# Mamba-2 block and quick-GELU layer: float64 weights in 1024-byte runs, held transfers, code pages shifted by idle products, y in two parts, w_out stationary in one group

## Chip, cores, metric

One Trainium2 chip, one of its cores. The metric is the device time of one execution in microseconds (us). Lower is better.

## What is computed

Two layers. The first is a state-space (SSD) recurrence over 4 batches x 8 heads x 768 positions, head size 32, state size 16. The second is a feed-forward layer over the 3072 tokens that come out, 256 to 2048 to 256 wide, with h / (1 + exp(-1.702 h)) between. Cut to what matters:

```python
# per batch and head; x 32 wide, B and C 16 wide
state = decay * state + B[j] x[j]          # decay from a
y[i] = C[i] . state                        # (done by chunks)
x = y as (3072, 256)
h = x @ w_in                               # (256, 2048)
g = h * sigmoid(1.702 * h)
out = g @ w_out                            # (2048, 256)
```

`w_in` and `w_out` arrive as float64; everything else is float32. The kernel turns the float64 bits into float32 on the chip.

## The kernel before

**Tiling.** The 3072 tokens are six groups g = 0 to 5 of 512; a group is two pairs of 256 tokens (PG = 2). The title's counting begins at 1, the code's at 0: "group 1" is g = 0, "groups 2 and 3" are g = 1 and 2. Each group goes through: the SSD part for its two pairs (`decay`, `score`, `weigh`, `gain`, `keep_both`, `finish`, which leaves y in `yT`), the hidden layer (16 blocks f of 128 columns), and the projection.

**SSD names.** `decay(p)` scans the decays into `L` on DVE, from rows of a that `spread(p)` broadcasts from a scratch tensor in DRAM into a tile of the `bits` pool. `score` multiplies C and B into `cb` (PE, L666), `weigh` is L times cb (DVE, L677), `gain` makes the increments A of the state (PE, L697) from x and `Be`, and `finish` makes y: an inter-chunk part (PE, L787) and an intra-chunk part (PE, L799). Its two pieces are 64 and 128 small matmuls of at most 64 columns. The first group has forms of its own: `mask_banks` (L534), `differ` (L540), `decay_exp`, `since_first`, `parts_first`, `keep_first` (a scan on DVE, L721).

**Weights.** `PIECES` lists four pieces of w_in with 2 blocks, two with 4, and four of w_out with 4. `fetch(i)` brings one piece as raw 32-bit words into a tile of the `bits` pool (four buffers). DVE and ACT then make float32 of it: `fields` (two DVE operations, L188 and L191), `clamp` (two on ACT, L199 and L200), `rounded` (DVE, L204), `join` (two on DVE, L215 and L221; L221 writes `w_in` or `w_out`). `narrow(i)` is `rounded(i)`, `fields(i+1)`, `join(i)`.

**Group g = 0** is computed plainly: `hidden(0, f)` is two products of 128x512 (L846), `project_all` sums over f with gT stationary and w_out moving (L944), four products of 128x256 for each f, and two DVE operations (L950) scale the result for `store`. **From g = 1 on** both layers work on 2x2 blocks with seven products in place of eight: `first` (L902, L912) with the mixed tiles `mix_in` and `mix_y`, and `product` (L1009, L1016) with `mix_w` and `mix_g`; `combine` and `turn_out` (transposes on DVE, L1063) make the output. In g = 1 the first four hidden blocks are plain too (steps H0 and H1).

**Order.** The order of every engine is that of the code, pinned by `in_order`. It is written by hand: lists of steps such as `"2.1 3.1 2.5 ... y L"`, in which "j.i" is product i of block j, "P" the next product of the group before, "D", "S", "T" the DVE and ACT steps of a block, and other names call functions; and `at(places, f, ...)`, which puts work behind a block. All loads but a few of the first are issued from SP in that order, so a load that waits holds back what stands behind it on SP.

**Idle products.** `keep_busy(4, 20)` runs 20 products of 32x32 and 4 of 128x192 on constants before the first real ones. In `product`, for g = 1 the first 30 products run as two halves of 128 columns.

In the head, the SP order before is: a, C, B, `fetch(0)`, x of pairs 0 and 1, `fetch(1)` to `fetch(3)`, all of a (`rows_a`), `fetch(4)`, `fetch(5)`; later `load(PG)`, which is b, c and x of pair 2.

Of the kernel before, what the change touches and what calls it, by code (L numbers as in the profile page):

```python
# [16 lines left out]
P = 128  # L17
# [18 lines left out]
def kernel(  # L36
# [73 lines left out]
    w_in = const.tile([P, NK, DF], FP32, name="w_in")  # L110
    w_out = const.tile([P, NF, DM], FP32, name="w_out")
# [51 lines left out]
    def fetch(i):  # L163
        name, f, n = PIECES[i]
        if n == 2 and f % 4:
            t = pieces.pop(i - 1)[:, 2 * n * DM:]
        else:
            t = pieces[i] = words(f"bits{i}")
            t = t[:, :2 * n * DM]
        if name == "in":  # L170
            src = moe_w_in[:, 2 * f * P:2 * (f + n) * P].rearrange("(k p) e -> p k e", p=P)
            dst = t.rearrange("p (k e) -> p k e", k=NK)
        else:
            src = moe_w_out[f * P:(f + n) * P, :].rearrange("(f p) e -> p f e", p=P)
            dst = t.rearrange("p (f e) -> p f e", f=n)
        nc.sync.dma_start(out=dst, in_=src)
        t = t.rearrange("p (e w) -> p e w", w=2)
        bits[i] = t[:, :, 0], t[:, :, 1]
# [32 lines left out]
    def join(i):  # L211
# [5 lines left out]
        if name == "in":  # L217
            dst, split = w_in[:, :, f * P:(f + n) * P], NK
        else:
            dst, split = w_out[:, f:f + n, :], n  # L220
        nc.vector.scalar_tensor_tensor(  # L221
            out=dst, in0=m.bitcast(FP32).rearrange("p (k e) -> p k e", k=split),
            scalar=2.0 ** -20, in1=p2.bitcast(FP32).rearrange("p (k e) -> p k e", k=split),
# [14 lines left out]
    def spread(p):  # L238
# [3 lines left out]
        else:  # L242
            ra[p] = words(f"a{p}").bitcast(FP32)[:, :2 * NH * H].rearrange(
                "p (k e) -> p k e", k=2)
        b, c = divmod(2 * p, NC)
# [38 lines left out]
    for i in range(1, 4):  # L284
        fetch(i)
    rows_a(az, (nc.sync,))
    for i in range(4, 6):
        fetch(i)
# [47 lines left out]
    for k in range(2):  # L336
        fold_ident(k)
# [37 lines left out]
    whose = const.tile([32, 1 + PG, NH, N], FP32, name="whose")  # L375
    nc.gpsimd.memset(whose, 1.0)
    for t, head in ((whose[:, 1:], PG), (whose[:, :1], 1)):
        nc.gpsimd.affine_select(out=t, in_=t, pattern=[[-1, t.shape[1]], [-head, NH], [0, N]],
                                compare_op=ALU.is_equal, fill=0.0, base=0, channel_multiplier=1)
# [43 lines left out]
    def keep_busy(n, m):  # L423

        t = bank("busy")
        for i in range(m):
            c = 32 * (i % R)
            nc.tensor.matmul(out=t[c:c + 32, :32], lhsT=ones[:32, :32], rhs=ones[:32, :32],
                             start=True, stop=True, tile_position=(0, c), skip_group_check=True)
        for i in range(n):  # L430
# [58 lines left out]
    def fan_rows(t, c0, c1, o):  # L489

        o = o[:, :(c1 - c0) * P]
        nc.tensor.matmul(out=o, lhsT=whose[:, 0].rearrange("p h n -> p (h n)"),
# [4 lines left out]
    def since_first():  # L497

        since[0] = ssd.tile([P, NC, P], FP32, tag="since", name="since0")
        o = bank("rows0")  # L500
        for p in range(PG):
            nc.tensor.matmul(out=o[:, 2 * p * P:2 * (p + 1) * P],
                             lhsT=whose[:, 1 + p].rearrange("p h n -> p (h n)"),
                             rhs=cum[:32].rearrange("p k s -> p (k s)"), start=True, stop=True,
                             tile_position=(0, 0), skip_group_check=True)
        to = since[0][:, :CG]
        nc.scalar.activation(to.rearrange("p c s -> p (c s)"), o, AF.Exp)
        nc.gpsimd.tensor_copy(
            drop[:, :, 1:], to.rearrange("p c (s i) -> p (c s) i", s=2)[:, 1:, H - 1].unsqueeze(
                1).to_broadcast([P, Q * D, 2 * CG - 1]))  # L510

    def fan_since():
# [3 lines left out]
        nc.tensor.matmul(out=f, lhsT=whose[:, 0].rearrange("p h n -> p (h n)"),  # L516
# [244 lines left out]
    def finish(pairs):  # L761
# [4 lines left out]
        y = area(f"y{pairs[0]}")[:, :, :len(pairs) * 2 * H].rearrange(  # L766
            "p (s t) (k i) -> p s t k i", s=2, i=H)
        both, y = y, [y[:, i] for i in range(2)]
        begun = set()
# [45 lines left out]
        else:  # L815
            for part in inter, intra:
                for n, p in enumerate(pairs):
                    part(n, p)
# [21 lines left out]
    def hidden(g, f):  # L840
# [4 lines left out]
        for k in range(NK):  # L845
            nc.tensor.matmul(out=h, lhsT=w_in[:, k, f * P:(f + 1) * P], rhs=yT[g][:, k],  # L846
                             start=(k == 0), stop=(k == NK - 1))
# [6 lines left out]
    def mix_in(n):  # L854
# [3 lines left out]
        w = w_in[:, :, 4 * n * P:4 * (n + 1) * P].rearrange(  # L858
            "p k (j i e) -> p k j i e", j=2, i=2)
        a11, a12, a21, a22 = w[:, 0, :, 0], w[:, 1, :, 0], w[:, 0, :, 1], w[:, 1, :, 1]  # L860
# [20 lines left out]
    def first(g, j, i):  # L881
# [6 lines left out]
        A = w_in[:, :, 2 * j * P:2 * (j + 1) * P].rearrange("p k (i e) -> p k i e", i=2)  # L888
# [48 lines left out]
    def project_all(g, between):  # L937

        o = [bank(f"o{g}_{j}").rearrange("p (k e) -> p k e", k=2) for j in range(CG // 2)]
        for f in range(NF):  # L940
            for do in between.get(f, []):
                do()
            for k in range(CG):
                nc.tensor.matmul(out=o[k // 2][:, k % 2],  # L944
                                 lhsT=gT[g, f // 2][:, f % 2, k * P:(k + 1) * P],
                                 rhs=w_out[:, f], start=(f == 0 and k % 2 == 0),
                                 stop=(f == NF - 1), skip_group_check=True)
        for half in range(2):
            ob = out_tile(g, half)
            nc.vector.tensor_single_scalar(out=ob, in_=o[half], scalar=1.0 / GELU_SCALE,  # L950
                                           op=ALU.mult)
            store(g, half, ob)
# [429 lines left out]
```

## Time and profile before

| | us |
|---|---|
| median of 5 runs | 360.34 |
| lowest to highest | 357.21 to 363.61 |
| the profiled execution | 358.18 |
| its span, first to last instruction | 356.4 |
| mean granted TensorE clock | 0.986 |

The page is one execution. Times in it are us unless they are marked ns, counted from the first instruction. PE is TensorE, PEld its weight loads, DVE VectorE, ACT ScalarE, POOL GpSimd, SP the engine that issues most transfers. An fp32 product shows as two records on PE. "issue" is time in which an engine waited for nothing that the profile shows. q1 is the queue of SP's transfers, q8 carries instructions. The page's slices of 8.9 us:

```profile
PE   8589999999999999989999999999999999999996
DVE  6869997999696999677789285789384455465463
PEclk9959999999999999999999999999999999999999
DMA  5987399532655000476214503210000210000301
```

Each digit is a tenth of the slice. PE is busy nearly everywhere, the second and third slices apart, and in the third the granted clock is half. The transfers are thick in the first 60 us.

### The profile page before, as it was taken

How to read it: one execution, taken by the hardware profiler on the slowest of the kernel's cores; microseconds unless marked ns; L12 is line 12 of the kernel's file. 1: busy time of each engine (PE TensorE's matmuls, PEld its weight loads, DVE VectorE, ACT ScalarE, POOL GpSimd, SP SyncE). 2: the span in 40 equal slices, each digit the busy share in tenths (PEclk: the TensorE clock that was granted, in tenths of full speed). 3: DMA queues.
4: the chain of work that ended last, by engine and by line, in shares of the span. 5: the costliest groups of instructions: out<-in, count | busy, mean ns of one | idle time of the engine just before them, and what ended most of it. 6: DMA issues, size and time to landing. Idle time of an engine off the chain costs nothing.

```text
span 356.4 us, 8330 instructions
## 1 busy us (share of the span) xinstructions
PE 345.4 (97%) x3516; PEld 286.6 (80%) x3516; DVE 255.7 (72%) x476; ACT 148.0 (42%) x329; POOL 14.5 (4%) x40
## 2 busy tenths in 40 slices
PE   8589999999999999989999999999999999999996
PEld 6354448887679998868888888888888888889996
DVE  6869997999696999677789285789384455465463
ACT  4748756103363431635333445333444331453320
POOL 8400000100000100000000000000000000000000
PEclk9959999999999999999999999999999999999999
DMA  5987399532655000476214503210000210000301
GB/s 144 243 282 160 122 213 260 97 78 33 138 131 105 2 0 2 73 132 109 36 26 78 100 5 89 37 23 2 1 4 2 37 24 0 1 2 0 61 0 59
DMA packets 81533, 25.92 MB, mean 73 GB/s; under 512 B 69081, under 2 KB 75097, under 8 KB 81497
## 3 DMA queue, kind: packets, MB, share of 16 engines
q1 hardware_dynamic: 80824, 25.01, 32.0%
q8 instruction: 27, 0.44, 0.5%
q10 hardware_dynamic: 672, 0.39, 0.4%
q14 instruction: 10, 0.07, 0.1%
HBM read 22.15 MB, written 3.24 MB: 71 GB/s over the span
## 4 chain that ended last, share of the span: by engine, by line
PE 95%; DVE 2%; issue 1%; ACT 1%; DVEq 0%
PE acc L1009 27%; PE X L902 18%; PE Y L912 13%; PE h L846 11%; PE o L944 8%; PE acc L1016 7%; PE y L799 3%; PE y L787 2%; PE cb L666 2%; PE A L697 1%; PE busy L431 1%; DVE L L677 1%; PE ab L534 0%; PE ab L540 0%; DVE c L1040 0%
## 5 line engine op out<-in xcount | busy, mean ns | idle before, releaser
L907 ACT ACTIVATE ac<-X 128x256 f32<-128x256 f32 x76 | 29.1, 382 | 81.4 <-PE X L902 81.0
L1009 PE MATMUL acc<-mg,mw 128*128 128x256 f32 (+1 forms) x216 | 54.7, 356 | 0.0
L1036 DVE TENSOR_TENSOR gT<-Y,ac 128x512 f32<-128x512 f32 x38 | 26.2, 689 | 37.0 <-PE Y L912 32.7
L879 ACT ACTIVATE gT<-gT 128x512 f32<-128x512 f32 (+1 forms) x76 | 39.3, 520 | 32.3 <-DVE gT L1036 31.6
L902 PE MATMUL X<-my,mi 128*128 128x256 f32 x152 | 45.1, 380 | 0.0
L1009 PEld LDWEIGHTS acc<-mg,mw 128*128 128x128 f32 x216 | 39.0, 190 | 4.8
L1036 DVE TENSOR_TENSOR gT<-Y,b 128x256 f32<-128x256 f32 x38 | 15.9, 419 | 31.8 <-PE Y L912 31.8
L846 PE MATMUL h<-yT,w_in 128*128 128x512 f32 x80 | 37.7, 632 | 0.7 <-ACT yT L822 0.7
L1009 PE MATMUL acc<-gT,w_out 128*128 128x256 f32 (+1 forms) x148 | 35.6, 351 | 0.0
L846 PEld LDWEIGHTS h<-yT,w_in 128*128 128x128 f32 x80 | 16.1, 203 | 20.3 <-issue 18.1
L902 PEld LDWEIGHTS X<-my,mi 128*128 128x128 f32 x152 | 27.5, 190 | 3.2
L1009 PEld LDWEIGHTS acc<-gT,w_out 128*128 128x128 f32 x148 | 26.2, 190 | 3.2
L944 PE MATMUL o<-w_out,gT 128*128 128x256 f32 x128 | 28.5, 381 | 0.0
L870 DVE TENSOR_TENSOR mg<-gT 128x512 f32<-128x512 f32 x40 | 27.2, 681 | 0.0
L944 PEld LDWEIGHTS o<-w_out,gT 128*128 128x128 f32 x128 | 24.0, 190 | 3.3 <-issue 0.2
L902 PE MATMUL X<-yT,w_in 128*128 128x256 f32 x76 | 23.3, 390 | 0.0
L907 ACT ACTIVATE b<-X 128x256 f32<-128x256 f32 x38 | 14.6, 383 | 20.8 <-PE X L902 20.3
L912 PE MATMUL Y<-yT,mi 128*128 128x256 f32 x76 | 22.7, 381 | 0.3 <-DVE gT L1036 0.3
L912 PE MATMUL Y<-my,mi 128*128 128x256 f32 x76 | 22.7, 381 | 0.1
L912 PE MATMUL Y<-yT,w_in 128*128 128x256 f32 x76 | 22.6, 379 | 0.0
L902 PE MATMUL X<-my,w_in 128*128 128x256 f32 x76 | 22.5, 380 | 0.0
L397 DVE TENSOR_TENSOR_SCAN L<-a,idents 128x1024 f32<-128x1024 f32 x9 | 20.5, 2282 | 0.0
(151 smaller groups left out, 545.2 us busy)
## 6 DMA issues: line engine op xcount, KB each, us to landing
a<-scratch SPq DMA_DIRECT2D x18, 256.0 KB, 6.2
bits<-in_moe_w_out_dram SPq DMA_DIRECT2D x4, 1024.0 KB, 6.0
x<-in_x_dram SPq DMA_DIRECT2D x24, 128.0 KB, 3.0
bits<-in_moe_w_in_dram SPq DMA_DIRECT2D x4, 512.0 KB, 5.3
bits<-in_moe_w_in_dram SPq DMA_DIRECT2D x2, 1024.0 KB
out_dram<-ob SPq DMA_DIRECT2D x32, 64.0 KB, 1.9
b<-in_B_dram SPq DMA_DIRECT2D x20, 64.0 KB, 2.5
af<-in_a_dram SPq DMA_DIRECT2D x3, 384.0 KB
```

The costliest lines, as they stand in the source:

```text
L397: nc.vector.tensor_tensor_scan(out=L, data0=ra[p].rearrange("p k e -> p (k e)"), data1=idents.rearrange("p h i -> p (h i)"), initial=0.0, ...
L799: nc.tensor.matmul(out=y[i][D * q:D * q + D, t, 2 * n + k], lhsT=rx[p][side, k, h], rhs=L[side, k, h // Q, h % Q], start=begin(i, t, (q,)) ...
L846: nc.tensor.matmul(out=h, lhsT=w_in[:, k, f * P:(f + 1) * P], rhs=yT[g][:, k], start=(k == 0), stop=(k == NK - 1))
L870: nc.vector.tensor_tensor(out=t[:, 0:2], in0=B[:, :, 1], in1=B[:, 0], op=ALU.subtract)
L879: nc.scalar.activation(o, i, AF.Silu, scale=GELU_SCALE)
L902: nc.tensor.matmul(out=s["X"], lhsT=lhsT, rhs=rhs, start=i == "1", stop=i == "4", skip_group_check=True)
L907: nc.scalar.activation(copy, s["X"], AF.Copy)
L912: nc.tensor.matmul(out=o, lhsT=lhsT, rhs=rhs, start=s.pop("new", False), stop=i != "5", skip_group_check=True)
L944: nc.tensor.matmul(out=o[k // 2][:, k % 2], lhsT=gT[g, f // 2][:, f % 2, k * P:(k + 1) * P], rhs=w_out[:, f], start=(f == 0 and k % 2 == 0 ...
L1009: nc.tensor.matmul(out=acc[g][0][i][:, cols], lhsT=w, rhs=h[:, cols], start=(j == 0 and k == 0 and (i, 0) in begins), stop=(j == NF // 2 - ...
L1016: nc.tensor.matmul(out=o[k] if type(o) is list else o[:, cols], lhsT=h[:, cols], rhs=w, start=(j == 0 and (i, k) in begins), stop=(j == NF ...
L1036: nc.vector.tensor_tensor(out=o, in0=v, in1=w, op=ALU.add)
```

## The change

- *1024-byte runs.* `w_in` lies as [P, NF, NK, P] and `w_out` as [P, 2, NF, P]. `fetch` makes two transfers of a piece, each in runs of 256 words; `join` writes the new places, and the readers (`hidden`, `mix_in`, `first`, `mix_w`, `product`) address them.
- *Held transfers.* `fetch(i, held=True)` and `spread(p, held=True)` first set a column of their tile by a DVE memset, so that the transfer waits for that place in DVE's order. `fetch(1)` to `fetch(5)` and `rows_a` are now issued after `weigh(0)` (the first held), b and c of pair 2 ahead of them, its x later. In g = 1, `more_loads` comes later and its first spread is held; from g = 2 on, the spread and `spread_rows` that opened the group are behind y, held, and `along` (clip and scan of the rows) is behind block 5.
- *Idle products.* `keep_busy(4, 45)`, and `pads(11, busy)` ahead of the last mask. The halved products of `product` in g = 1 are the first 5 in place of 30; of the first hidden products of g = 1, six run in four parts and two in halves.
- *First group's SSD.* `since_first` uses two strips of 32 rows and two banks, with two ACT operations. The copy into `drop` goes from POOL to DVE, after `weigh(1)`. `fold_ident(1)` comes after the transposes, `rounded(0)` right after `fields(0)`.
- *y in two parts.* `finish(pairs, steps)` can run its inter and intra parts apart: for g = 1 at f = 13 and f = 15 of `project_all`, for g = 2 at "z" and "y" of the list. `mix_y(1)` comes behind f = 15. What stood behind H1 (`gain`, `score`, `keep_both`, `weigh`) stands behind H0, with the second `weigh`.
- *w_out stationary.* `project_all` for g = 0 has w_out stationary and 512 columns of gT moving, two products for each f. The result comes out transposed; two ACT copies scale it into `sums`, and `turn_out(0, 0)` and `(0, 1)` behind H1 transpose and store it.

```diff
-    w_in = const.tile([P, NK, DF], FP32, name="w_in")
-    w_out = const.tile([P, NF, DM], FP32, name="w_out")
+    w_in = const.tile([P, NF, NK, P], FP32, name="w_in")
+    w_out = const.tile([P, 2, NF, P], FP32, name="w_out")
...
+        if held:
+            nc.vector.memset(t[:, :1], 0)
         if name == "in":
             src = moe_w_in[:, 2 * f * P:2 * (f + n) * P].rearrange("(k p) e -> p k e", p=P)
-            dst = t.rearrange("p (k e) -> p k e", k=NK)
+            dst, src = (v.rearrange(s, h=n, e=2 * P) for v, s in (
+                (t, "p (h k e) -> k p h e"), (src, "p k (h e) -> k p h e")))
         else:
-            src = moe_w_out[f * P:(f + n) * P, :].rearrange("(f p) e -> p f e", p=P)
-            dst = t.rearrange("p (f e) -> p f e", f=n)
-        nc.sync.dma_start(out=dst, in_=src)
+            src = moe_w_out[f * P:(f + n) * P, :].rearrange("(f p) (h e) -> h p f e", p=P, h=2)
+            dst = t.rearrange("p (h f e) -> h p f e", h=2, f=n)
+        for k in range(2):
+            nc.sync.dma_start(out=dst[k], in_=src[k])
...
     load(1, "x")
-    for i in range(1, 4):
-        fetch(i)
-    rows_a(az, (nc.sync,))
-    for i in range(4, 6):
-        fetch(i)
+    load(PG, "bc")
...
-    for k in range(2):
-        fold_ident(k)
+    fold_ident(0)
...
+    def pads(n, t):
+        for i in range(n):
             c = 32 * (i % R)
             nc.tensor.matmul(out=t[c:c + 32, :32], lhsT=ones[:32, :32], rhs=ones[:32, :32],
                              start=True, stop=True, tile_position=(0, c), skip_group_check=True)
...
+    def drops():
+        nc.vector.tensor_copy(
+            drop[:, :, 1:], since[0][:, :CG].rearrange("p c (s i) -> p (c s) i", s=2)[:, 1:, H - 1].unsqueeze(
                 1).to_broadcast([P, Q * D, 2 * CG - 1]))
...
         for k in range(NK):
-            nc.tensor.matmul(out=h, lhsT=w_in[:, k, f * P:(f + 1) * P], rhs=yT[g][:, k],
-                             start=(k == 0), stop=(k == NK - 1))
+            n = 2 if g == 1 and NK * f + k < 14 else 1
+            if n == 2 and NK * f + k < 14 - 8:
+                n = 4
+            for e in range(n):
+                cols = slice(e * TG // n, (e + 1) * TG // n)
+                nc.tensor.matmul(out=h[:, cols], lhsT=w_in[:, f, k], rhs=yT[g][:, k, cols],
...
-            for k in range(CG):
-                nc.tensor.matmul(out=o[k // 2][:, k % 2],
-                                 lhsT=gT[g, f // 2][:, f % 2, k * P:(k + 1) * P],
-                                 rhs=w_out[:, f], start=(f == 0 and k % 2 == 0),
+            for c in range(2):
+                nc.tensor.matmul(out=o[c], lhsT=w_out[:, c, f],
+                                 rhs=gT[g, f // 2][:, f % 2], start=(f == 0),
...
-                n = 2 if g == 1 and 7 * j + ORDER.index(i) < 30 else 1
+                n = 2 if g == 1 and 7 * j + ORDER.index(i) < 5 else 1
...
-    keep_busy(4, 20)
+    busy = bank("busy")
+    keep_busy(4, 45)
     both = area("ab0")
     for r in range(R):
         mask_banks(0, r, both[:, r])
     for r in range(R):
+        if r == R - 1:
+            pads(11, busy)
         mask_banks(1, r, bank(f"ab1_{r}"))
     turn_first("C")
     turn_first("B")
+    fold_ident(1)
...
     fields(0)
+    rounded(0)
     clamp(0)
     score(range(PG), turn_back)
     ends_first(0)
     ends_first(1)
     since_first()
     weigh(0)
+    fetch(1, held=True)
+    for i in range(2, 6):
+        fetch(i)
+    rows_a(az, (nc.sync,))
     weigh(1)
-    rounded(0)
+    drops()
...
-    at(in_project[0], 13, lambda: finish(pairs))
-    at(in_project[0], 14, lambda: mix_in(1), lambda: mix_in(2), lambda: mix_in(3),
-       lambda: turn_blocks(2), lambda: mix_y(1), lambda: decay(n))
+    at(in_project[0], 13, lambda: finish(pairs, (0,)))
+    at(in_project[0], 15, lambda: finish(pairs, (1,)))
+    at(in_project[0], 13, lambda: mix_in(1), lambda: mix_in(2), lambda: mix_in(3),
+       lambda: turn_blocks(2), lambda: decay(n))
+    at(in_project[0], 15, lambda: mix_y(1))
...
     at(after, "H0", lambda: decay(n + 1), lambda: since_start(n),
-       lambda: since_start(n + 1))
-    at(after, "H1", lambda: gain(later), lambda: score(later),
-       lambda: keep_both(later), lambda: weigh(n))
+       lambda: since_start(n + 1), lambda: gain(later), lambda: score(later),
+       lambda: keep_both(later), lambda: weigh(n), lambda: weigh(n + 1))
+    at(after, "H1", lambda: turn_out(0, 0), lambda: turn_out(0, 1))
...
     def more_loads():
-        spread(p)
+        spread(p, held=True)
...
         if most:
             load(p)
-            spread(p)
-            for b in rows:
-                spread_rows(b)
...
             if most:
+                spread(p, held=True)
+                for b in rows:
+                    spread_rows(b)
                 load(p + 1)
                 spread(p + 1)
```

## Prediction

> **What bounds the kernel now.** First the page's busy table and the chain that ended last:
>
> ```profile
> span 356.4 us, 8330 instructions
> PE 345.4 (97%) x3516; PEld 286.6 (80%) x3516; DVE 255.7 (72%) x476; ACT 148.0 (42%) x329; POOL 14.5 (4%) x40
> ...
> PE 95%; DVE 2%; issue 1%; ACT 1%; DVEq 0%
> ```
>
> PE sets the time. From the first product of the hidden layer at 21.97 to the end it runs back to back, so only three things can move the end: when that product starts, how fast PE is clocked, and PE's own work. Next, what PE waited for (total, times, longest), and the timeline around the longest wait (start, us, then the group):
>
> ```profile
> PE y L799 <- issue: 4.3, 2, 2.8
> ```
> ```profile
> 12.82 0.86 PE L697 MATMUL A<-x,Be 64*32 64x64 f32 x64
> 14.48 0.82 PE L799 MATMUL y<-L,x 64*32 64x64 f32 x61 [0.80 <-DVE L L677]
> 18.09 1.28 PE L799 MATMUL y<-L,x 64*32 64x64 f32 x67 [2.79 <-issue]
> 19.30 1.96 PE L787 MATMUL y<-CsT,steps 32*64 32x64 f32 x56
> ```
>
> In the middle of 128 small matmuls PE stops for 2.79 us with nothing to wait for. The queue table names the cause:
>
> ```profile
> q8 instruction: 27, 0.44, 0.5%
> ```
>
> 27 packets, 0.44 MB, so 16 KB each, for PE's 3516 matmuls and 3516 weight loads: 260 to a packet, 256 if an instruction has 64 bytes. Counting along PE's order, 349 matmuls and as many loads and some ten control instructions lie ahead of the first stop (15.30), 1874 ahead of the second (1.52 us at 157.56): both are about 60 instructions short of a multiple of 256 (the 3rd, the 15th). PE waits for its next page of code. The q8 packet that ends the first stop starts between 15.5 and 15.7, and PE goes on at 18.09. The windows (busy us of PE, PEld, DVE, ACT and POOL; then granted clock, DMA share, GB/s) show what the stops cost and what the fetch competed with:
>
> ```profile
> 3.00:5.00 2.00, 2.00 (x8) 1.75 (x8) 1.96 (x5) 0.64 (x2) 1.80 (x5) 1.00 0.69 183
> 13.00:17.00 4.00, 1.50 (x125) 1.22 (x111) 4.00 (x5) 3.29 (x7) 3.41 (x3) 1.00 1.01 357
> 17.16:27.40 10.24, 8.59 (x130) 5.13 (x130) 6.93 (x14) 4.34 (x7) 0.37 (x2) 0.50 0.89 278
> 157.10:160.50 3.40, 1.88 (x114) 1.58 (x99) 0.95 (x2) 0.43 (x1) 0.00 (x0) 1.00 0.45 98
> ```
>
> After the first stop the clock is 0.50 until 27.40; after the second it stays 1.00. From 21.97 to 27.40 hidden products ran at half speed: 5.4/2 = 2.7 us lost.
>
> **The head, step by step.** *Idle products.* 25 more at the start and 11 before the last mask are 72 records; 40 took 0.76, so 19 ns each, 1.4 us. PE had no slack there (the masks end at 6.54, just when L540 begins), so the ab products, both exponentials, cb, Be and weigh all come later; I take 1.2, ends 1.0 and 1.4. What they buy: the page boundary that stood at the 91st y product moves to the 19th, the one before it from A to the end of cb. With the 60 instructions of lead, page 3 is now needed at A's 53rd product and page 4 at y's 117th.
>
> *Transfers held back.* The five w_in pieces go behind a one-element memset after weigh(0) (DVE, 13.2 before, 14.4 now), so SP issues them at about 14.5 and they flow about 2 us later (before: issued 10.70, a window at 13.00 full of them). Behind the waiting DMA on SP stand only the rest of the weights and rows_a (needed at 36.5); the b and c of pair 2 go ahead of it. Page 3 is then asked near 12.3 and page 4 near 15.6, both ahead of the weights. A quiet fetch I size by the second stop: the inter products start at 155.78, PE goes on at 159.08, 3.3. So page 3 comes at 15.2 to 15.6 (A's last 11 products wait 1 us), page 4 at 18.5 to 18.9.
>
> *The chain behind A.* rows in two strips saves about 0.5 of its 1.13, hidden by Be. A ends near 15.4; four ACT copies 1.28; the L721 scan 1.68, which ends at 18.4 (16.76 before). `drop` moves from POOL (0.96) to DVE and fits while DVE waits for the copies; rounded(0) (0.85) moves into the 1.23 that DVE idled before Be; the second half of idents goes behind the transposes, where DVE waited 0.94 for the weights. The inter products run from 18.7 (page 4 and scan together) for 1.05 at full clock, yT 0.65: **hidden starts at about 20.4 instead of 21.97**, 1.6 earlier.
>
> *The clock.* A rule weighed: the Trainium skill, "TensorE: Matmul & The Clock Gate", Part 1, has PE fall to half clock after an idle window of about 3.4 us. Read literally, a gap of 2.79 would not drop it and removing that gap would win nothing here; the row says it did, with PE busy for 0.82 of the 3.41 us ahead of 17.16 (24%), while 1.88 of 3.40 (55%) at 157.10 left it alone. The new gaps (1 us in A, 1.5 in y) leave PE busy about half of any 3.4 us. By the row I take full clock: 2.7 won; by the other reading 0.
>
> *Then DVE.* w_in is turned to float32 on DVE, and this pipeline has slack now only because PE was late:
>
> ```profile
> 23.80 0.69 DVE L215 SCALAR_TENSOR_TENSOR p<-bits,p 128x512 uint32<-128x512 uint32 x1 [3.17 <-ACT p L200]
> ...
> 35.35 1.23 DVE L221 SCALAR_TENSOR_TENSOR w_in<-m,p 128x1024 f32<-128x1024 f32 x1
> ```
>
> From the scan's end (16.76) to join(4) (36.58) are 19.8 us, of which 3.2 idle for ACT, which sat behind yT: 16.6 of work. From 18.4 that gives 35.0. hidden(0, 8) would be due at 20.4 + 16 x 0.86 = 34.2, so PE waits 0.8 there. Before, it started at 38.3: the head keeps **3.3**. Behind it DVE has slack (o block 8 needs w_out 5.4 us after it is there, block 12 4.7), and its 1.78 wait at 57.83 closes.
>
> *1024-byte runs.* A second rule against the rows: "DMA: Bandwidth & Descriptors", Specifications, gives 512 bytes as enough for line rate. By it the pieces land as fast as before. The windows say otherwise: 183/0.69 = 265 GB/s in 1024-byte runs (B and C), 357/1.01 = 353 in w_in's 2048. 3.67 MB then take 13.9 us against 10: with flow from 16.5 the last piece is there at 30.6, by the rule at 27. DVE wants it at about 31 (fields(5), ahead of join(4)); the others have 0.5 to 1 us to spare. So nothing by either, but the row leaves no margin; end 1.5 lost. What short runs give is a shorter turn for a code page between weight runs (the same page, arbitration: an engine drains a whole packet of one ring before the next); no run here sizes it.
>
> **The rest.** *w_out stationary in g = 0:* 64 products of 0.432 (16 records, 3.46) become 32 of 0.86: 0.1 won. The two L950 (1.28, DVE) become two ACT copies in its idle time; two transposes of 0.70 (L1063) and eight stores come after H1, where DVE idled 2.5 and 2.7. *Splits:* 25 of 30 halved acc products become whole, 0.448 to 0.432, 0.4 won; six hidden products in four parts, at 8 x 0.112, lose 0.25. *y in two parts, mix_y later, H0 before the rest:* gain() now comes two hidden blocks earlier (3.4) and its Be of the second pair would be about 0.5 late; the 0.34 wait of Y on gT at 102.13 goes, as weigh has H1 as cover. -0.2. *Held spreads:* the memset of L sits where DVE idled 2.69 (107.2), decay(p) follows at 113.5 and a lands 6.2 after issue: just in time. In g = 2 `a` and `af` leave the stop at 157.56 alone. The boundaries from the 14th on stay where they were (one product off), so that stop stays; a fetch without company is 2.9 (its packet 0.5 after asking, as at the quiet y of 265) instead of 3.3: 0.4 won. Ends for all of this: -1 and +1.5.
>
> **Sum.** 3.3 + 0.1 + 0.4 - 0.25 - 0.2 + 0.4 = 3.75, on 358.18 (span 356.4 and 1.8 around it): 354.4. The median of the five is 360.34, 2.2 above the profiled one: runs with a worse first stop are likely among them, and these gain more. I add 0.6 and carry 4.35 over: **356.0**.
>
> **Rivals.**
> 1. *The clock drops all the same* (the two gaps fall in one window of the gate). For it: busy is only about half. Hidden starts 1.6 earlier, half speed to about 27.4: 0.8 won at hidden 8, DVE no bound, 0.4 for the rest: 1.2, 359.1.
> 2. *Code pages come in time altogether* (asked earlier than I think): A ends 0.9 earlier, the scan 17.5, join(4) 34.1: 4.2 + 0.45 + 0.6 = 5.3, 355.0; with an `af` stop gone too, 353.8.
> 3. *Slower: page 4 meets the weights.* It is asked at 15.6, the weights flow from 16.5; it decides if the ask is more than 0.9 later or the flow that much earlier. The page of 18.1 started only at 22.51 in before, 4.4 later, under full DMA. Then page 4 starts at 20, PE goes on at 22.4, inter at half clock ends 24.5, hidden starts 25.3 and is cold to about 31: hidden 8 at 25.3 + 13.8 + 2.9 = 42.0, 3.7 late, less 0.4: 363.6, to 365 with late weights. Against it: the short runs.
> 4. *The placing does nothing* (pages are not what PE waited for): 1.2 lost on pads, 0.4 won: 361.1. Against it: two stops at the same distance from a boundary, each with its packet.
>
> **How the numbers follow.** About 1% (3.6 us) is what a measurement can tell. Chances: forecast 0.48, rival 1 0.20, rival 2 0.18, rival 3 0.10, rival 4 0.04. The forecast's own ends (pads 0.2, fetch 0.5, weights 1.5, rest 1.5) give 353 to 359, 0.62 of it past 1%; with rival 2 nearly whole and a tenth of rival 1 faster is 0.50, raised to 0.55 because the median hides worse runs; slower is rival 3 and little more, 0.09; same 0.36. Range 351 to 361.5: rivals 1, 2 and 4 within, rival 3 out.
>
> **What would show it.** Hidden's first product at 20 to 21, clock 1.00 from 17 to 27, join(4) ending near 35 with a wait of PE for DVE there, "issue" waits of about 1 us in A and y, and still 1.1 at the y of g = 2. Wrong if the first product starts at 22 or later, if the clock row again has ten us of 0.50, or if PE waits for w_in at several blocks.

## The result, and the profile after

| | before | after |
|---|---|---|
| median, us (runs) | 357.59 (80) | 354.59 (43) |
| profiled execution, its span | 358.18, 356.4 | 354.80, 353.1 |
| mean granted clock of that execution | 0.986 | 0.990 |
| ratio, 95% interval | | 0.9935 [0.9921, 0.9949] |
| ratio again, beside experiments 5 to 7 (22 runs) | | 0.9938 [0.9914, 0.9963] |

The change makes the kernel 0.65% faster, 2.3 us: a gain, but within the 1% that the forecast set as its bound. Ratios leave out runs over 1.5% above the fastest of their kernel, 19 of 80 before and 1 of 43 after, so that the medians (3.0 us apart) and the means of all runs but three of 590 us and more (358.1 and 354.8, 3.3 apart) show more than the ratio.

The page after, its first lines, the granted clock in 40 slices of 8.8 us, and the chain that ended last:

```profile
span 353.1 us, 8361 instructions
PE 345.3 (98%) x3514; PEld 276.7 (78%) x3514; DVE 254.8 (72%) x481; ACT 149.0 (42%) x332; POOL 12.2 (3%) x40
...
PEclk9969999999999999999999999999999999999999
...
PE 93%; DMA 2%; DVE 2%; issue 1%; SPq 1%; ACT 0%; DVEq 0%
```

PE is busy for the same 345 us. The clock row still has a 6 in the third slice, where before had a 5. What PE waited for (total, times, longest):

```profile
PE y L814 <- issue: 1.1, 1, 1.1
PE y L814 <- DVE L L689: 0.9, 1, 0.9
PE h L868 <- ACT yT L839: 0.7, 1, 0.7
```

Of the two "issue" waits in y, 4.3 us together, one of 1.1 is left. It is the one in the head; the timeline (start, us, group, in brackets the idle time before it) has it where it was to be, at the 117th y product (places such as this one are counted in PE's records, two for one float32 product):

```profile
13.02 1.33 PE L709 MATMUL A<-x,Be 64*32 64x64 f32 x64
15.23 1.37 PE L814 MATMUL y<-L,x 64*32 64x64 f32 x117 [0.88 <-DVE L L689]
17.67 0.33 PE L814 MATMUL y<-L,x 64*32 64x64 f32 x11 [1.06 <-issue]
17.93 1.96 PE L802 MATMUL y<-CsT,steps 32*64 32x64 f32 x56
20.60 3.78 PE L868 MATMUL h<-yT,w_in 128*128 128x512 f32 x4 [0.72 <-ACT yT L839]
```

A takes 1.33 in place of 0.86: the page before it. Hidden starts at 20.60. But its first four records, two products of 128x512, take 3.78, which is half speed. The windows (busy PE, PEld, DVE, ACT, POOL; clock, DMA share, GB/s), cut where the granted clock changes:

```profile
16.19:19.60 3.41, 2.35 (x110) 2.11 (x92) 2.15 (x3) 1.03 (x2) 0.00 (x0) 1.00 0.68 178
19.60:23.01 3.41, 2.69 (x11) 1.27 (x8) 1.46 (x3) 2.42 (x4) 0.00 (x0) 0.50 0.95 269
23.01:26.42 3.41, 3.41 (x5) 1.35 (x4) 2.53 (x5) 1.93 (x3) 0.00 (x0) 0.50 0.97 314
```

6.8 us at half clock (it is 1.00 again from 26.42), after a window in which PE was busy for 2.35 of 3.41 us (69%). DVE meanwhile waits for weights, and piece 4 is joined at 36.45, not 35.0:

```profile
20.12 0.43 DVE L192 TENSOR_SCALAR p<-bits 128x512 uint32<-128x512 uint32 x1 [1.74 <-DMA bits<-in_moe_w_in_dram]
...
23.86 0.43 DVE L192 TENSOR_SCALAR p<-bits 128x512 uint32<-128x512 uint32 x1 [2.24 <-DMA bits<-in_moe_w_in_dram]
...
35.22 1.23 DVE L225 SCALAR_TENSOR_TENSOR w_in<-m,p 128x1024 f32<-128x1024 f32 x1
```

And the y of g = 2, in before and then in after:

```profile
159.08 0.95 PE L799 MATMUL y<-L,x 64*32 64x64 f32 x70 [1.52 <-issue]
```
```profile
155.09 1.57 PE L814 MATMUL y<-L,x 64*32 64x64 f32 x128
```

The stop that the forecast kept, at 1.1 us, is gone altogether: the 128 records run in one piece. Stage by stage the two profiles differ like this (starts on PE, us):

| stage starts | before | after | won here |
|---|---|---|---|
| hidden, g = 0 | 21.97 | 20.60 | 1.37 |
| the ab products behind hidden block 9 | 42.02 | 40.85 | -0.20 |
| hidden, g = 1 | 87.05 | 85.92 | -0.04 |
| A behind g = 1 | 133.97 | 132.31 | 0.53 |
| cb of the third group (g = 2's list) | 151.43 | 149.77 | 0.00 |
| the next A | 189.08 | 185.71 | 1.71 |
| end of the span | 356.4 | 353.1 | -0.07 |

Two profiles are two executions, and the experiments show how far the head moves from one to the next.

### The profile page after: what moved, and what is told of

It is laid out like the page before. It is cut to its first block, busy times and chain, and to the rows that moved or that the text cites. A ratio compares the mean times of both kernels' runs of the same rounds, so it can differ in the third digit from the quotient of the medians.

```text
span 353.1 us, 8361 instructions
## 1 busy us (share of the span) xinstructions
PE 345.3 (98%) x3514; PEld 276.7 (78%) x3514; DVE 254.8 (72%) x481; ACT 149.0 (42%) x332; POOL 12.2 (3%) x40
## 3 DMA queue, kind: packets, MB, share of 16 engines
q1 hardware_dynamic: 89272, 25.02, 33.3%
## 4 chain that ended last, share of the span: by engine, by line
PE 93%; DMA 2%; DVE 2%; issue 1%; SPq 1%; ACT 0%; DVEq 0%
PE acc L1029 28%; PE X L924 18%; PE Y L934 14%; PE h L868 11%; PE o L966 8%; PE acc L1036 7%; PE y L814 3%; PE y L802 2%; PE cb L678 2%; DMA zC<-in_C_dram 1%; PE A L709 1%; DMA bits<-in_moe_w_in_dram 1%; DVE L L689 1%; SPq L274 0%; DVE c L1060 0%
## 5 line engine op out<-in xcount | busy, mean ns | idle before, releaser
L1029 PEld LDWEIGHTS acc<-mg,mw 128*128 128x128 f32 x196 | 36.7, 190 | 4.8
L868 PE MATMUL h<-yT,w_in 128*128 128x512 f32 (+2 forms) x120 | 38.4, 480 | 0.7 <-ACT yT L839 0.7
L868 PEld LDWEIGHTS h<-yT,w_in 128*128 128x128 f32 x120 | 20.1, 200 | 17.9 <-issue 15.8
L966 PE MATMUL o<-gT,w_out 128*128 128x512 f32 x64 | 28.6, 597 | 0.0
L1029 PEld LDWEIGHTS acc<-gT,w_out 128*128 128x128 f32 x132 | 24.5, 190 | 3.4 <-ACT yT L841 0.2
L966 PEld LDWEIGHTS o<-gT,w_out 128*128 128x128 f32 x64 | 11.8, 190 | 13.2 <-issue 12.8
```

The source lines that it names most:

```text
L868: nc.tensor.matmul(out=h[:, cols], lhsT=w_in[:, f, k], rhs=yT[g][:, k, cols], start=(k == 0 and e == 0), stop=(k == NK - 1), skip_group_ch ...
L966: nc.tensor.matmul(out=o[c], lhsT=w_out[:, c, f], rhs=gT[g, f // 2][:, f % 2], start=(f == 0), stop=(f == NF - 1), skip_group_check=True)
L1029: nc.tensor.matmul(out=acc[g][0][i][:, cols], lhsT=w, rhs=h[:, cols], start=(j == 0 and k == 0 and (i, 0) in begins), stop=(j == NF // 2 - ...
```

## The experiments

Three sets, each on one chip with the kernel before beside it: 1 to 4 (its median 357.89 there), then 5, 6, the first run of 7, and 11 (357.43), then the second run of 7, and 8 to 10 (357.17). Ratios are to the kernel before in the same set.

### 1. The held spreads of g = 2 and later undone

```diff
         if most:
             load(p)
+            spread(p)
+            for b in rows:
+                spread_rows(b)
...
         def refill():
             if most:
-                spread(p, held=True)
-                for b in rows:
-                    spread_rows(b)
```

> The changed kernel with one part undone: from g = 2 on, the spread and the rows of a are issued at the opening of the group again, not held; the place of along stays. PE's instructions and their page boundaries are the same. Theory (the code page of that y had to queue behind the transfers of a and af, and moving them is what took the 1.52 us stop away): an issue wait of about 1.5 us in the y of g = 2 is back, its q8 packet starts near the y instead of 5 us ahead of it, and the time is 1.4 to 1.7 us above the changed kernel. Rival (the stop went because boundaries or waits ahead of y moved): no stop, time within 0.3 us of the changed kernel.

Measured: median 357.15, ratio 0.9993 [0.9963, 1.0022]. The y of the third group in its timeline:

```profile
155.15 0.81 PE L814 MATMUL y<-L,x 64*32 64x64 f32 x59
157.73 0.92 PE L814 MATMUL y<-L,x 64*32 64x64 f32 x69 [1.77 <-issue]
```

The stop is back and the gain is gone: without this part, the rest of the change is worth nothing that can be measured. From A to A, around this y, it takes 55.3 us as in before (55.1), against 53.4 after. The trace has the code page's packet start 5.4 us after cb begins (before: 5.3; after: 1.7).

### 2. The idle products put elsewhere

```diff
-    keep_busy(4, 45)
+    keep_busy(4, 20)
...
-        if r == R - 1:
-            pads(11, busy)
...
     finish(range(PG))
+    pads(36, bank("late"))
```

> The changed kernel with its 36 added idle products run behind the first group's y instead of at the start (20 at the start as before), so that only the page boundaries of the head go back; all later ones stay. Theory (the pads cost 0.8 us in the head, where PE starts ab at 7.26 instead of 6.46, and with the transfers held the pages come quietly anyway): the ab products start at 6.5, the first hidden product at 20.0 to 20.6 although the pads now take up to 0.7 after y, and the time is within 0.5 us of the changed kernel. Rival (the placing is what shortens the stops): the stop of 2 us or more in y is back, the first hidden product starts at 21.5 or later and the time is 1 us or more above the changed kernel.

Measured: 355.18, ratio 0.9926 [0.9894, 0.9958]. Its timeline:

```profile
16.34 0.90 PE L814 MATMUL y<-L,x 64*32 64x64 f32 x67 [0.77 <-issue]
...
21.00 1.12 PE L430 MATMUL late<-ones 32*32 32x32 f32 x67 [1.74 <-issue]
```

The y stop is now where before had it, at the 61st product, only 0.77 long; but a second page falls due at the sixth of the pads' records, and costs 1.74, so that hidden starts at 22.05 and not at the 20.0 to 20.6 that was expected. The ratio is still the changed kernel's. The place of a stop moves with the pads, which rules out rival 4; that this place is better than before's is not shown by it.

### 3. Dense products in the two gaps of the head

Four products of 128x192 on constants behind `gain` and four behind `finish`.

```diff
     gain(range(PG))
+    dense(4)
...
     finish(range(PG))
+    dense(4)
```

> The changed kernel with eight idle products of 128x192 in PE's two gaps of the head, four ahead of y (where PE waits 0.88 for L) and four behind y (where it waits 0.72 for yT). Theory (the clock falls because the products of the head are small ones that keep the array little busy, so dense work in the same gaps holds it; but with a full clock the weights are late: w_in's pieces are there at 20.1 and 23.9): the mean granted clock rises from 0.990 towards 0.995 to 1.0, PE then waits for w_in from DVE for 1.5 to 2.5 us, and the time is within 0.6 us of the changed kernel. Rival (the weights are no bound, the forecast's sum): the clock stays up and the time falls by 2 us or more. Third: the clock falls all the same, no change in the time.

Measured: 356.84, ratio 0.9993 [0.9971, 1.0014]. The clock never falls in its profile, and from hidden's start to ab it takes 18.5 us in place of 20.25. But (its waits):

```profile
PE y L814 <- issue: 2.4, 2, 1.4
...
PE h L868 <- DVE w_in L225: 1.0, 1, 1.0
```

The wait for w_in is at hidden(0, 8), which the forecast had at 0.8 for a head at full clock. The second "issue" wait, 1.4, is at the last y (it goes on at 264.32): eight more products, 16 records, moved a later page boundary into it. So holding the clock is possible, and over all 22 runs the mean clock is 0.997. The stage is 1.75 shorter with the wait for w_in already inside it. The gain went elsewhere: hidden starts 1.2 later than in after (0.6 of that is there at the ab products, before any dense product), and 1.4 goes at the last y.

### 4. The transfers not held

```diff
+    for i in range(1, 4):
+        fetch(i)
+    rows_a(az, (nc.sync,))
+    for i in range(4, 6):
+        fetch(i)
...
-    fetch(1, held=True)
-    for i in range(2, 6):
-        fetch(i)
-    rows_a(az, (nc.sync,))
```

> The changed kernel with the transfers of the head not held: w_in's pieces 1 to 5 and the rows of a are issued right behind x, ahead of the b and c of pair 2, as before. Theory (the hold is what lets the code pages of the head through): the pages of A and y meet the weights, the issue wait in y grows from 1.06 to 3 us or more, the first hidden product starts at 22 or later and the time is 1 to 2.5 us above the changed kernel. Rival (the hold costs as much as it gives, since the weights come late): the pieces are there 3 us earlier, and the time is equal or lower by up to 1 us.

Measured: 355.58, ratio 0.9928 [0.9905, 0.9952]. In its timeline

```profile
19.14 0.33 PE L819 MATMUL y<-L,x 64*32 64x64 f32 x11 [2.16 <-issue]
```

the stop doubles, as the page starts at 16.72 in place of 14.68, and hidden starts at 22.08. On the other side DVE waits 0.6 us for weights in place of 4.5. The ratio is the changed kernel's, within two intervals of 0.25%, but the median is 1.0 us higher in another set, and the mean clock over its 21 runs is 0.9889, where after has 0.9924. What would make up for the later page is not shown: PE waits for no weights in either profile.

### 5. w_in in long runs again

```diff
-    w_in = const.tile([P, NF, NK, P], FP32, name="w_in")
+    w_in = const.tile([P, NK, DF], FP32, name="w_in")
...
-            dst, src = (v.rearrange(s, h=n, e=2 * P) for v, s in (
-                (t, "p (h k e) -> k p h e"), (src, "p k (h e) -> k p h e")))
+            dst, src = t.rearrange("p (k e) -> k p e", k=NK), src.rearrange("p k e -> k p e")
```

(and the readers of w_in accordingly)

> The changed kernel with one thing undone: w_in lies as before and its pieces come in runs of 2048 and 4096 bytes, in two transfers each. Theory A (short runs bring the code pages nothing, and make the weights late, which the half clock hides): the time equals the changed kernel's within 0.4 us; the two waits of the vector engine for the pieces (1.74 and 2.24 us) shrink to under 1 in sum, the last piece of w_in is joined 2 to 3 us earlier than 36.4; the stop in the y products stays near 1.1 us and the code page after it does not start more than 1 us later than the 3.6 us it takes in the changed kernel. Theory B (short runs are what lets a code page through): the stop in y, or one in the first hidden products, grows by 1.5 us or more, and the time by 1 us or more.

Measured: 355.20, ratio 0.9944 [0.9919, 0.9969]; on the same chip the changed kernel 354.50 and 0.9938. Timeline and the waits of DVE:

```profile
20.07 0.36 PE L813 MATMUL y<-L,x 64*32 64x64 f32 x11 [3.28 <-issue]
```
```profile
DVE p L191 <- DMA bits<-in_moe_w_in_dram: 1.5, 2, 1.0
```

The same wait in after, and in number 6, which has long runs too:

```profile
DVE p L192 <- DMA bits<-in_moe_w_in_dram: 4.5, 3, 2.2
```
```profile
DVE p L191 <- DMA bits<-in_moe_w_in_dram: 2.6, 2, 1.8
```

Both theories have a part. With long runs DVE's wait for w_in is 1.5 in place of 4.5, and the page started at 17.81 in place of 14.68 or 15.90 (the two profiles of after). But the last early piece is joined no sooner (36.97; DVE now waits 3.1 for ACT), and the time differs by no more than the intervals. That short runs let a page through sooner is seen in one profile of a quantity that moves by some us from run to run (below); it isn't settled. Nor does the length of the runs alone set the wait: 2.6 in number 6.

### 6. Dense products, long runs, and the later pages kept in place

Number 3 with number 5, and eight products fewer among the split hidden products of g = 1, so that PE issues 3514 records again.

```diff
-            if n == 2 and NK * f + k < 14 - 8:
+            if n == 2 and NK * f + k < 2:
                 n = 4
```

> The run with dense products behind gain and behind finish, and two things more: w_in in long runs, and eight products fewer in the split hidden products of the next group, so that every later code page begins where it does in the changed kernel. Theory A (dense fill keeps the clock, and what it then cost was the late weights, 1.0, and a page boundary moved onto the last y, 1.4): no wait of the tensor engine for w_in over 0.3 us, no stop at the last y, no clock below 0.9 from 15 us on; about 352.5 us of profiled time, 1.5 to 2.5 below the changed kernel. Theory B (the dense products themselves and the pads cost what the clock gives): within 0.7 us of the changed kernel.

Measured: 353.83 (10 runs), ratio 0.9927 [0.9898, 0.9955]; span 351.6, clock 1.0. Of its waits, the one that is left of those above, and two lines of its timeline:

```profile
PE y L813 <- issue: 1.0, 1, 1.0
```
```profile
22.21 17.33 PE L867 MATMUL h<-yT,w_in 128*128 128x512 f32 x40
39.47 0.69 PE L409 MATMUL ab<-X,ones 32*64 32x256 f32 x16
```

The forty hidden records (twenty products) now take 17.3 us, ab starts 1.4 earlier than after although hidden starts 1.6 later, and the wait for w_in and the stop at the last y are gone. Its interval lies wholly below number 3's, so those two did eat the gain there. The mean clock over its ten runs is 0.999. Beside the changed kernel it is 0.7 us lower in the median and 1.5 in the profile: the best version here, not one that the intervals separate.

### 7. The held spreads alone, on the kernel before (twice)

```diff
         if most:
             load(p)
-            spread(p)
-            for b in rows:
-                spread_rows(b)
...
             if most:
+                spread(p, held=True)
+                for b in rows:
+                    spread_rows(b)
                 load(p + 1)
```

(`along` moves behind block 5, as in the change)

> The kernel before with one part of the change alone: from the third group on, the spread of the decays (and of their rows) is held until behind y, and the scan of the rows is behind block 5. Theory A (this part carries nearly all of the gain, since the code page at the y of the third group no longer stands behind these transfers): the stop of 1.52 us there is gone, the stop of 2.79 us in the head is as before, and the time is 1.5 to 2.2 us below the kernel before, that is, within 0.5 us of the changed kernel. Theory B (the gain is the sum of head and rest as forecast, 3.3 and 0.5): 0.4 to 0.8 us below the kernel before, and the stop is shortened by at most 0.5.

Measured: 356.26, ratio 0.9983 [0.9958, 1.0008]. The stage from A to A is 53.4 us as in after, and the stop there is gone; yet the gain of the ratio is 0.6: the stop as in theory A, the time as in theory B. So once more:

> The kernel before with the held spreads alone, once more: its profile shows the stop of the third group gone and that stage 1.7 us shorter, yet its median lies only 1.2 below the kernel before and the ratio is 0.9983. Theory A (the part is worth 1.7 in every run and the first measurement was unlucky in the head): ratio 0.995 to 0.997. Theory B (in part of the runs the kernel before has no stop there): again 0.998 or above.

Measured: 356.02, ratio 0.9981 [0.9960, 1.0003]. The same again, 0.7 us by the ratio and 1.2 in the medians, so not ill luck. By the ratios of both sets this part alone is worth about 0.7 of the 2.3; what it lacks to the 1.7 of its profile is taken up below. The second profile's head, in order:

```profile
16.53 0.90 PE L801 MATMUL y<-L,x 64*32 64x64 f32 x67 [1.54 <-issue]
...
19.98 1.98 PE L848 MATMUL h<-yT,w_in 128*128 128x512 f32 x4 [0.72 <-ACT yT L824]
23.94 1.45 PE L848 MATMUL h<-yT,w_in 128*128 128x512 f32 x3 [1.97 <-issue]
```

Two stops, 3.5 us together, and no loss of clock: ab at 39.48, earlier than in any profile of the changed kernel. The first profile of the same code had one stop of 5.12 in y.

### 8. The kernel before, a second profile

> The kernel before, for a second profile: how much the two stops vary from run to run. If the stop at the y of the third group belongs to the kernel it is 1.3 to 1.9 us again; if the stop in the head depends on how the transfers fall it differs by over 1 us from 2.79 (a kernel with the same head had 5.1).

Two lines of its timeline, the head and the third group (span 354.3, clock 0.99, one run of 356.11):

```profile
16.70 0.90 PE L799 MATMUL y<-L,x 64*32 64x64 f32 x67 [1.70 <-issue]
...
157.01 0.95 PE L799 MATMUL y<-L,x 64*32 64x64 f32 x70 [1.08 <-issue]
```

The stop of the third group is there again, 1.08 against 1.52; that of the head is 1.70 against 2.79. With the same head, four profiles (two of before, two of number 7) have 2.79, 1.70, 5.12 and 1.54: the trace on which the forecast stood showed one draw.

### 9. Only the decays' spread at the opening, the rows behind y

```diff
             load(p)
+            spread(p)
...
             if most:
-                spread(p, held=True)
                 for b in rows:
                     spread_rows(b)
```

> The changed kernel with the spread of the decays (two transfers of 256 KB) back at the opening of each group from the third on, while the rows of a (384 KB) stay behind y. Theory A (any of these transfers in flight when the page is asked holds it up; the two of the decays come first and are what the page meets): a stop of 1 to 1.9 us at the y of the third group, time within 1 us of the kernel before. Theory B (the rows of 3072-byte runs, later in the queue, are what the page stands behind): no stop over 0.3 us there, time within 0.5 us of the changed kernel.

Measured: 358.60, ratio 1.0020 [0.9991, 1.0050].

```profile
159.15 0.92 PE L814 MATMUL y<-L,x 64*32 64x64 f32 x69 [0.42 <-issue]
```

The page starts 4.1 us after cb begins: 2.4 more than in after, 1.3 less than with the rows too. So in this profile the two transfers of 256 KB are the larger part of what holds it up. The stop in this profile is 0.42, between the theories, while the time is as bad as number 1's or worse. Why it is no better than number 1 stays open; its head in the profile was a bad draw as well (a stop of 2.71).

### 10. Number 6 without the idle products

```diff
-    keep_busy(4, 45)
+    keep_busy(4, 20)
...
-            pads(11, busy)
...
-    dense(4)
+    dense(2)
```

(the second fill; 36 products are given back as halves and quarters in g = 1)

> The run with dense products, long runs of w_in and kept page places, and in the head three things more: the 36 idle pads taken out (25 at the start, 11 ahead of the last mask), the second dense fill two products long in place of four, and the 36 products given back behind the head as halved and quartered products of the second group, so that the code pages of the third group and later begin where they do in the changed kernel. Theory A (pads cost 0.8 to 1.3 us in the chain behind the masks and buy nothing, since a stop in y comes all the same): the scan ends 0.8 us earlier, one stop of 0.7 to 1.1 in y, no half clock, hidden starts near 20.8, ab of the first hidden blocks near 38.5 against 39.5, 0.4 lost on the split products: about 351 us of span, 0.3 to 0.8 below the run with the pads. Theory B (the pads keep a second stop out of the head): a stop of 1 us or more falls into the inter products or the first hidden ones, and the time is 0.5 to 1.5 us above the run with pads.

Measured: 355.88, ratio 0.9988 [0.9965, 1.0012]. Its waits:

```profile
PE y L801 <- issue: 1.9, 1, 1.9
...
PE y L813 <- issue: 1.0, 1, 1.0
```

This is theory B. A starts earlier (12.25), and then the page due at the 53rd y product and the next one at the 53rd inter product both stop PE, 1.0 and 1.86, and the clock is half for one window behind that. The interval lies above number 6's. So there the pads seem to earn more than they cost, but the run also halves the second fill and splits more products of g = 1, and these were not tried apart.

### 11. The changed kernel again

> The changed kernel as it is, on the same chip as the three others, so that differences under one microsecond can be read: ratio 0.992 to 0.995 to the kernel before. The stop in the y products of the head at about the 117th of them and 1.0 to 1.1 us long, the clock at half for 5 to 9 us around the first hidden products or not at all, as the windows of the clock gate happen to fall.

Measured: 354.50, ratio 0.9938. A second profile of it has the y stop at the 117th product and 1.49 long, one window of half clock (21.61 to 25.02), hidden at 21.64 and ab at 40.70.

## Where the forecast was right, and where it failed

The forecast was 356.0 us, a ratio of 0.988 to the median of 360.34 that it stood on. The median came out at 354.6 and the ratio at 0.9935, because that 360.34 was a high five: 80 runs have 357.59. Half of the expected 1.2% is there. That the time lies so near the forecast is partly luck: the base was 2.75 too high, the 2.7 of the clock did not come in the profile, and the third group and the opening of g = 1 gave 1.9 more than forecast. "Faster by over 1%" had 0.55 and did not come; "within 1%" did.

- **What bounds the kernel, and the code pages: right.** The stop stood at the 117th y product as counted, 1.06 long (forecast 1.5), A was stretched by 0.47 (1; by 0.12 or nothing in six other profiles with these pads), and hidden started at 20.60 (20.4; 21.64 in the second profile). A page holds 256 instructions here: 72 more records ahead moved the boundary from the 61st y record to the 117th, and 61 - 72 + 128 is 117, 128 records with as many weight loads. Pads cost 0.8 up to the ab products in this profile and 1.1 to 1.6 in the seven others that have all of them at the start (7.58 to 8.07 in place of 6.46; forecast 1.2).
- **Inter products: mis-sized.** 1.05 at full clock was the forecast; they take 1.96 at full clock as at half. Their rate is not set by the clock.
- **The clock: the step that failed.** 2.7 was to be won. In the two profiles nothing was: 5.4 us of hidden at half speed before, 5.8 after (5.2 and 3.4 in the second profiles). The row used, 55% busy at 157.10 with no drop, did not carry over: 69% dropped it in the head. Nor is it one threshold of busy time: in number 7's second profile PE is busy 1.70, 2.69 and 1.44 of three windows cut at 14.00 and keeps 1.00 (wherever the windows are cut, one has at most 1.95):

```profile
14.00:17.41 3.41, 1.70 (x132) 1.49 (x132) 3.41 (x4) 2.15 (x5) 3.25 (x4) 1.00 1.03 366
17.41:20.82 3.41, 2.69 (x60) 2.21 (x59) 2.86 (x7) 1.49 (x3) 0.00 (x0) 1.00 1.03 272
20.82:24.23 3.41, 1.44 (x4) 0.57 (x3) 2.38 (x5) 2.74 (x5) 0.00 (x0) 1.00 1.05 394
```

And in after's second profile a window with 1.86 busy left the clock alone, while behind the next, with 2.17, it fell. The rule set beside it (the Trainium skill, "TensorE: Matmul & The Clock Gate", Part 1) has idle windows of 3.4 us that run freely against the kernel. The free running fits: in all eleven profiles with half clock the stretch is 10.24, 6.83 or 3.41 us, three, two or one of such windows, and it begins anywhere from 17.16 to 22.41. An idle window does not: the one of 16.19 was two thirds busy, though with products of 64x64 and smaller. Dense products in the same gaps kept the clock (numbers 3 and 6); whether small products count for less was not tried by itself.

- **What the clock step is worth in the mean.** Each run has a mean granted clock. It is 0.9880 for before (the 137 runs that the ratios use), 0.9884 for the spreads alone (36) and 0.9924 for after (65). 0.0040 x 355 us = 1.4 us of lost time less, where 2.7 was forecast. The medians of the last two differ by 1.5, their means by 1.1. So the head's parts together gain about that, and fewer windows at half clock are enough to account for it. It is a reading of means, and the profile of after had two windows. Number 4 points to the hold as the part that does it: without the hold the mean is 0.9889.
- **The head's 3.3: 1.2 in the first two profiles.** With the clock at half, hidden gave back 0.2 of its 1.4. In the second two it is -0.3 (the ab products at 40.40 before and 40.70 after). So a pair of profiles does not show what the head gains; the means above are the better measure.
- **DVE and the weights: the size right, the cause in part missed.** The forecast had the short runs cost nothing and DVE busy from the scan to join(4). DVE waited 4.5 us, half clock hid it, and with full clock it showed as 1.0 at hidden(0, 8). The size of that wait was right (0.8 forecast); part of its cause is the weights' coming, which the forecast had put at nothing. In number 6, with long runs, it was gone. But the row that the forecast set against the rule of 512 bytes as enough for line rate (the Trainium skill, "DMA: Bandwidth & Descriptors", Specifications), 265 GB/s for 1024-byte runs, did not carry over. Here is a window of after, in 1024-byte runs but for its end, and one of number 6, in long runs:

```profile
26.42:29.83 3.41, 3.41 (x9) 1.52 (x8) 3.38 (x8) 2.46 (x5) 0.00 (x0) 1.00 1.11 389
```
```profile
23.80:27.20 3.40, 3.40 (x9) 1.52 (x8) 3.33 (x7) 2.73 (x6) 0.00 (x0) 1.00 0.99 384
```

From 25 to 29 it is 386 GB/s in after and 404 in number 6; from 19 to 25, when the first pieces come, both are slower, 266 and 279. So the rule fits these rows, and why DVE waits 4.5, 2.6 or 1.5 stays open.

- **The opening of g = 1: -0.05 forecast (0.4 - 0.25 - 0.2), 0.53 measured** (order, whole acc products, the wait of Y on gT gone; not taken apart). w_out stationary had 0.1, and its stage, from the ab products to hidden of g = 1, shows -0.04; it was not tried by itself.
- **The third group's stop: 0.4 forecast, 1.7 in the profile.** "That stop stays" was wrong. A boundary that does not move need not stop PE, if its packet starts early enough. The packet starts 1.4 to 2.4 us after cb in all eight kernels with held spreads and 4.6 to 5.4 with both spreads at the opening. The forecast sized the quiet case by another packet, the one at 265.78, which starts only when that y (265.17) has begun.
- **Sizes that do not add up.** By the ratios held spreads are worth 0.7 added to before and 2.0 taken from after, each within about 0.9. By the means of all runs they are worth 1.8 and 1.9 in number 7's two sets (standard error 0.4), beside 1.7 in its profile, and 3.0 taken from after (standard error 0.7), which lie closer together. The stop varies as well (1.08, 1.52, 1.77). And in the runs of its ratio number 1 has nearly after's mean clock (0.9918) with before's time. What makes these differences stays open.

Rival 1, the clock drops all the same, described the profile of the head best (1.2 won; it had 0.8 at hidden 8). Rival 3's late page did occur, in single executions of numbers 9 and 5: stops of 2.7 and 3.3.

## What to carry to other kernels

When an engine stops in a run of very small instructions with nothing to wait for, look for its code packet and for what transfers are in flight when that is asked: moving bulk transfers behind the spot cost PE no time and removed a stop of 1.1 to 1.8 us. Do not size a stop or a clock loss from one profile: take a second one of the same kernel first, and read the mean granted clock over all runs. Filling a gap with dense products held the clock here (a mean of 0.997 and 0.999 against 0.992), but count what they do to every later page boundary, and to the engine that was waiting with slack behind them.

## What the chip showed that was not expected

- A stop for a page ends 2.2 to 3.0 us after its packet starts, in the 22 such stops of over 0.4 us in all fourteen profiles, whatever the traffic: a packet takes 0.9 to 1.6 us and PE goes on 1.1 to 1.6 later. The variable part is when the packet starts: 13.66 to 18.04 for the same page of the same head.
- The page that is said to be fetched behind the running one, at a cost "mostly hidden" (the Trainium skill, "Runtime: NRT & Kernel Launch", Instruction fetch mechanics), is not hidden in y: 117 records with their weight loads are 234 instructions in 1.4 us, half of what a page takes to come.
- Mean granted clocks come in steps, 0.976, 0.981, 0.986, 0.990, 0.995, 1.000: one window of 3.41 us at half clock is 0.0048 of 355 us. In number 7's second set ten runs at 0.986 have a median of 356.6 us and five at 0.990 one of 355.3: 1.3 for one window, of the 1.7 that half its time would be.
